# Cosine attention and a low-rank mixer: natural u of two batches by DMA transposes, an earlier mark for w_ch2, and seven more zero products

## The chip, the core and the metric

The kernel runs on one core of one Trainium2 chip. The time is device microseconds from the first to the last instruction, with what lies around it. Three timed runs of the kernel before took 311.78, 313.64 and 314.64 us (median 313.64). The profile is of one further execution.

TensorE multiplies matrices, VectorE and ScalarE do elementwise work and copies, GpSimd (POOL) some casts and the queue of the weight loads and most output writes, and SyncE (SP) issues nearly all other DMAs. Each engine works through its own instructions in order. DMA transposes are issued from SP.

## What is computed

Eight batches of attention with 8 heads, 576 positions and 64 features, in linear form with cosine weights, and then a mixer:

```python
q_p, k_p = phi(q, cos_w, sin_w), phi(k, cos_w, sin_w)   # relu, times cos and sin: 128 features
kv  = einsum('bhsf,bhsd->bhfd', k_p, v)
num = einsum('bhsf,bhfd->bhsd', q_p, kv)
den = einsum('bhsf,bhf->bhs', q_p, k_p.sum(axis=2))[..., None] + 1e-6
x   = (num / den).transpose(0, 2, 1, 3).reshape(8, 576, 512)

h   = x.transpose(0, 2, 1) @ U @ V            # rank 32, over positions
u   = x + h.transpose(0, 2, 1)
out = u + relu(u @ w_ch1) @ w_ch2             # 512 -> 2048 -> 512
```

Inputs and output are float32; products run in bfloat16 with float32 sums.

## The kernel before

**Tiling.** The 576 positions of a batch are four chunks of 128 (c = 0 to 3) and a tail of 64 (c = 4). The tails of two batches share one tile. The channel product of a batch therefore has 16 slots of g1 (`g1_main`: one block of 128 hidden channels by 512 positions, four matmuls into `g_ps`, ScalarE's relu into `hid`), and for each pair of batches there are four slots of g1 for the tails (`g1_tail`) and 36 slots of g2 (`g2_part`: nine position chunks in four parts, four matmuls into `o_ps` each; after the last part VectorE adds u from `u_bf` into `o_sb`, and it is written out).

**u is needed twice.** Transposed (`uT`, channels on partitions) it is the moving operand of g1. Natural (`u_bf`, positions on partitions) it is the term added to the output at the end of g2. For batches 2 to 7, `u_unit` makes natural u (one matmul of V by A into `va_ps`, and VectorE's add of x), and `utr_dma` (line 455) makes `uT` of it with DMA transposes. For batches 0 and 1, which have no earlier work to hide such a transfer behind, `uT` is made straight in PSUM: `uTd_open` or `open_mm` multiplies x by the identity, `uTd_mm` adds the product of A and V, and `uTd_evac` copies the sum as bfloat16 to `uT`. Natural u of these two batches is then also made by `u_unit`, from the same x and A.

**Order.** It is written out by hand as a list of slots; thunks placed with `at(j, ...)` or `put(j, ...)` are issued after slot j. Slots 0 to 15 are g1 of batch 0, 16 to 31 the early g2 of batch 0 (part by part over four chunks), 32 to 47 g1 of batch 1, 48 to 51 the tails, 52 to 71 the rest of g2 of the first pair. Attention of the next batches is laid beside these slots; `PLAN` (line 624) gives for batches 2 to 7 where q, k and v are prepared, where `kv_unit`, `x_unit`, `A_unit` and `u_unit` go and where the next batch's loads are issued. Attention of batch 1 lies beside slots 0 to 45, that of batch 2 has its kv products at slots 46 and 48, that of batch 3 at 60 and 62.

**Natural u of batches 0 and 1.** Lines 853 to 854 put the four chunks of batch 0 after slots 5 to 8. Lines 874 to 875 put the tail pair's chunk after slot 32 and the four chunks of batch 1 after slots 42 to 45. PSUM buffers are those with the tag "o" (two).

**Queues.** SP issues, in this order: the loads of q, k and v of batches 0 and 1; at slot 15 a tiny DMA that reads `w2_bf` (`gate`, line 842, and line 898), so that SP waits there until the second quarter of w_ch2 has landed; the loads of batch 2; the transposes `uT_tl` (slot 33) and those of q of batch 2 (`qtr_dma`, slots 36 to 40); the loads of batch 3, and so on. POOL's queue loads w_ch1 and w_ch2 in four quarters each. A small copy on POOL ahead of each (lines 814 and 825) reads `vst`, so that POOL waits until v of batch 0, or of batch 1, has landed (the first half of its heads):

```python
G_.tensor_copy(out=mark, in_=vst[0:TS, 3, 4, 0:1])
for n in range(4):
    w2_load(n)
```

**The head.** Before q of batch 0 has landed, TensorE multiplies zeros (`keep_warm`, line 191; 13 products at line 790) into a buffer that nothing reads.

**Buffers that the change touches.** `uT` and `x_bf` have two buffers each, `u_bf` three.

Of the kernel before, what the change touches and what calls it, by code (L numbers as in the profile page):

```python
# [11 lines left out]
BF16 = mybir.dt.bfloat16  # L12
# [5 lines left out]
def kernel(  # L18
# [11 lines left out]
    nc = tc.nc  # L30
# [6 lines left out]
    P = 128  # L37
    DM = 512
# [4 lines left out]
    TS = 64  # L43
# [5 lines left out]
    def tail(b):  # L49
        lo = TS * (b % 2)  # L50
        return slice(lo, lo + TS)

    const = ctx.enter_context(tc.tile_pool(name="const", bufs=1))
    pool = ctx.enter_context(tc.tile_pool(name="work", bufs=2))
# [6 lines left out]
    kst = const.tile([P, H, 5, D], FP32)  # L61
    vst = const.tile([P, H, 5, D], FP32)
# [4 lines left out]
    def load_even(dst, src, b, h0=0, h1=H):  # L67
        nc.sync.dma_start(
            out=dst[0:P:2, h0:h1].rearrange("m h c d -> m h (c d)"),
            in_=nines(src, b)[:, h0:h1, 0 : 5 * D],  # L70
        )
# [20 lines left out]
    w2_bf = const.tile([P, NJ, DM], BF16)  # L92
# [20 lines left out]
    V_, A_, G_ = nc.vector, nc.scalar, nc.gpsimd  # L113
# [15 lines left out]
    def load_uv():  # L129
# [16 lines left out]
        out=iota[:, 0:4], pattern=[[2, 4]], base=0, channel_multiplier=9,  # L146
        allow_small_or_imprecise_dtypes=True,
    )
    for lo in (0, TS):
        nc.gpsimd.iota(  # L150
            out=iota[lo : lo + TS, 4:5], pattern=[[1, 1]], base=8, channel_multiplier=18,
# [3 lines left out]
        out=iota[:, 5:6], pattern=[[1, 1]], base=8, channel_multiplier=9,  # L155
# [6 lines left out]
        out=par, in_=ident[:, 1:P:2], op=ALU.add, axis=mybir.AxisListType.X  # L162
    )
    V_.tensor_scalar(
        out=iota[:, 0:4], in0=iota[:, 0:4], scalar1=par, scalar2=None, op0=ALU.add
# [24 lines left out]
    def keep_warm(n, tag, bufs):  # L190
        w_ps = ps.tile([P, 512], FP32, tag=tag, bufs=bufs, name="w_ps")
        for _ in range(n):
            nc.tensor.matmul(out=w_ps, lhsT=zero[:, 0:P], rhs=zero, start=True, stop=True)  # L193
# [3 lines left out]
    mark = const.tile([TS, 1], FP32)  # L197
# [36 lines left out]
    u_bf, u_tl, uT, uT_tl = {}, {}, {}, {}  # L234
# [51 lines left out]
    def k_of(b, c, h):  # L286
        return k_p[b][:, c, h, :] if c < 4 else k_tl[:, h, :]
# [20 lines left out]
    def qT_alloc(b):  # L308
        if b not in q_pT:
            q_pT[b] = pool.tile([P, 4, H, P], BF16, tag="q_pT", bufs=2, name="q_pT")  # L310
# [48 lines left out]
    def x_of(b, c, rows=slice(0, P)):  # L359
        return x_bf[b][:, c, :] if c < 4 else x_tl[rows, :]  # L360
# [22 lines left out]
    def x_unit(b, c, tag, bufs):  # L383
        x_alloc(b)
        n = P if c < 4 else TS
        rows = slice(0, P) if c < 4 else tail(b)
        acc = ps.tile([P, 2, 512], FP32, tag=tag, bufs=bufs, name="x_ps")
        for h in range(H):
            g, i = divmod(h, 4)
            nc.tensor.matmul(  # L390
                out=acc[:, g, i * E : i * E + E],
                lhsT=qT_of(b, c, h),
                rhs=kv_sb[b][:, h, :],
                start=True,
                stop=True,
            )
        view = acc[rows, :, 0 : 4 * E].rearrange("p g (i e) -> p g i e", e=E)
        rec = pool.tile([P, 2, 4], FP32, tag="rec", bufs=2, name="rec")
        recip(rec[rows], view[:, :, :, D])
        nc.vector.tensor_tensor(  # L400
            out=x_of(b, c, rows).rearrange("p (g i d) -> p g i d", g=2, d=D),
            in0=view[:, :, :, 0:D],
            in1=rec[rows].unsqueeze(3).to_broadcast([n, 2, 4, D]),
            op=ALU.mult,
        )

    def A_of(b):
        return A_sb[b % 4]
# [19 lines left out]
    def u_unit(b, c, tag, bufs):  # L428
        if b not in u_bf:
            u_bf[b] = pool.tile([P, 4, DM], BF16, tag="u_bf", bufs=3, name="u_bf")  # L430
        if c == 4:
            u_tl[b // 2] = pool.tile([P, DM], BF16, tag="u_tl", bufs=2, name="u_tl")
        va = ps.tile([P, DM], FP32, tag=tag, bufs=bufs, name="va_ps")
        if c < 4:
            nc.tensor.matmul(out=va, lhsT=V_bf[:, c, :], rhs=A_of(b), start=True, stop=True)  # L435
        else:
            for i in range(2):
                nc.tensor.matmul(  # L438
                    out=va[tail(i), :], lhsT=V_tl, rhs=A_of(b - 1 + i), start=True, stop=True,
                    tile_position=(0, i * TS),  # L440
                )
        nc.vector.tensor_tensor(  # L442
            out=u_bf[b][:, c, :] if c < 4 else u_tl[b // 2], in0=x_of(b, c), in1=va,
            op=ALU.add,
        )
# [9 lines left out]
    def utr_dma(b, c0, c1):  # L455
        if c0 < 4:
            uT_alloc(b)
            nc.sync.dma_start_transpose(
                out=uT[b][:, c0:c1, :, :].rearrange("m c d t -> m (c d) t"),
                in_=u_bf[b][:, c0:c1, :].rearrange("p c n -> p (c n)"),  # L460
            )
        else:
            uTt_alloc(b // 2)
            nc.sync.dma_start_transpose(out=uT_tl[b // 2], in_=u_tl[b // 2])

    uT_ps = {}

    def uTd_open(b, d, tag, bufs, t=None):
# [134 lines left out]
    def loads(b):  # L603
        def thunk(dst, src):
            def go():
                load_tail(dst, src, b)
                load_main(dst, src, b)

            return go

        return thunk(qst, q), thunk(kst, k), thunk(vst, v)

    ORD = (4, 0, 1, 2, 3)
# [58 lines left out]
    O2, G3 = ("o", 2), ("g", 3)  # L672
# [114 lines left out]

    FEATS = [(V_, V_ if c == 3 else A_) for c in TL]
    qT_alloc(0)
    keep_warm(13, "X", 1)  # L790
    t_q = []
    for c in TL:
        tg = G3 if c < 3 else O2
# [10 lines left out]
    for c in TL:  # L804
        k_prep(0, c, FEATS[c])
        for h in range(H):
            nc.tensor.matmul(
                out=z_ps[:, h : h + 1], lhsT=k_of(0, c, h), rhs=v_tl[:, 0, D:E],
# [13 lines left out]
    for h0 in (0, 4):  # L822
        load_odd(vst, v, 1, h0, h0 + 4)
        load_even(vst, v, 1, h0, h0 + 4)
    G_.tensor_copy(out=mark, in_=vst[0:TS, 3, 4, 0:1])
    for n in range(4):
        w2_load(n)
    g1_main(0, 0, True)
# [10 lines left out]
    def at(j, *thunks):  # L839
        beside.setdefault(j, []).extend(thunks)  # L840

    def gate(src):
        nc.sync.dma_start(out=mark2, in_=src)

    for n, c in enumerate(ORD):
# [4 lines left out]
        at(9 + n, lambda c=c: k_prep(1, c, (V_, A_)))  # L850
        at(15, lambda c=c, n=n: v_prep(1, 0, H, (c,), ((V_, V_, V_, V_, V_)[n],)))
        at(18 + 2 * n, lambda c=c: x_unit(1, c, "X", 1))
    for c in range(4):
        at(5 + c, lambda c=c: u_unit(0, c, *O2))
    for hg in range(2):
        at(16 + hg, lambda hg=hg: kv_unit(1, hg, "T", 1))

# [13 lines left out]
    at(27, lambda: A_unit(1, "T", 1, A_))  # L871
    at(28, open1)
    at(29, close1)
    for n, c in enumerate(ORD):
        at((32, 42, 43, 44, 45)[n], lambda c=c: u_unit(1, c, *O2))
    at(33, lambda: utr_dma(1, 4, 5))

    slots, todo = [], {}
# [16 lines left out]
    def put(at, thunk):  # L895
        todo.setdefault(at, []).append(thunk)

    put(15, lambda: gate(w2_bf[0:1, 4, 0:1]))
    for n, t in enumerate(loads(2)):
        put(15, t)  # L900
# [37 lines left out]
```

## Time and profile before

| what | value |
|---|---|
| timed runs | 311.78, 313.64, 314.64 us (median 313.64) |
| profiled execution, whole | 311.89 us |
| its span | 310.1 us |
| g2 products (`o_ps`, line 576) | 40% of the chain of waits |
| g1 products (`g_ps`, line 523) | 32% of the chain |
| natural-u products (`va_ps`, line 435), 32 in all | 2% of the chain |
| natural-u adds on VectorE (line 442), 32 in all | 21.8 us busy, 685 ns each |
| w_ch2 quarters, POOL's issues | 33.9 to 36.9 us |
| SP's small DMA on w_ch2 (line 843) | issued at 42.90 us |
| loads of batch 2, first issue | 43.77 us |

The page gives busy time by engine, the span in 40 slices of 7.75 us, the DMA queues, the chain that ended last, and groups of instructions with the idle time before them. Lines with "<-" in brackets name what ended an engine's idle time. A timeline line has start, duration, engine, line, operation, output and inputs, and how many were merged; SPq is SP's queue of DMA issues, and its durations are those of issuing, not of the transfer. PEld is the load of a matmul's weights, which overlaps the matmuls.

### The profile page before, as it was taken

How to read it: one execution, taken by the hardware profiler on the slowest of the kernel's cores; microseconds unless marked ns; L12 is line 12 of the kernel's file. 1: busy time of each engine (PE TensorE's matmuls, PEld its weight loads, DVE VectorE, ACT ScalarE, POOL GpSimd, SP SyncE). 2: the span in 40 equal slices, each digit the busy share in tenths (PEclk: the TensorE clock that was granted, in tenths of full speed). 3: DMA queues.
4: the chain of work that ended last, by engine and by line, in shares of the span. 5: the costliest groups of instructions: out<-in, count | busy, mean ns of one | idle time of the engine just before them, and what ended most of it. 6: DMA issues, size and time to landing. Idle time of an engine off the chain costs nothing.

```text
span 310.1 us, 5750 instructions
## 1 busy us (share of the span) xinstructions
PE 301.9 (97%) x2341; PEld 157.7 (51%) x2341; DVE 155.0 (50%) x342; ACT 136.0 (44%) x229; POOL 52.9 (17%) x96
## 2 busy tenths in 40 slices
PE   5999999999999999999999999999999999999995
PEld 1676454446655444574455444574455444474443
DVE  4979834896878584146327583046426520002111
ACT  2936730264820466679300366669300366640000
POOL 8410400510131008004221300003321000000000
PEclk9999999999999999999999999999999999999999
DMA  7999999979997979982999879912981240001131
GB/s 216 354 258 255 197 187 274 326 143 241 288 191 142 314 133 251 243 242 82 180 212 322 207 127 234 273 47 53 194 154 60 75 80 0 0 2 68 70 101 68
DMA packets 86027, 53.21 MB, mean 172 GB/s; under 512 B 54258, under 2 KB 83218, under 8 KB 86002
## 3 DMA queue, kind: packets, MB, share of 16 engines
q1 hardware_dynamic: 79298, 41.36, 57.5%
q0 software_dynamic: 6560, 11.43, 15.0%
q8 instruction: 18, 0.29, 0.4%
q10 hardware_dynamic: 144, 0.07, 0.1%
q14 instruction: 7, 0.06, 0.0%
HBM read 36.86 MB, written 9.44 MB: 149 GB/s over the span
## 4 chain that ended last, share of the span: by engine, by line
PE 90%; DVE 5%; DMA 2%; issue 1%; ACT 0%; ACTq 0%; DVEq 0%
PE o_ps L576 40%; PE g_ps L523 32%; PE gt_ps L543 5%; PE kv_ps L299 3%; PE x_ps L390 3%; PE va_ps L435 2%; DMA qst<-in_q_dram 2%; DVE q_p L260 2%; DVE k_p L260 2%; PE a_ps L415 1%; PE t_ps L328 1%; PE t_ps L316 1%; PE w_ps L193 0%; PE va_ps L438 0%; PE xh_ps L688 0%
## 5 line engine op out<-in xcount | busy, mean ns | idle before, releaser
L532 ACT ACTIVATE hid<-g_ps 128x512 bf16<-128x512 f32 x128 | 76.2, 598 | 106.2 <-PE g_ps L523 106.2
L576 PE MATMUL o_ps<-w_bf,hid 128*128 128x512 bf16 (+2 forms) x528 | 120.0, 372 | 0.0
L523 PE MATMUL g_ps<-uT,w_bf 128*128 128x512 bf16 x512 | 117.6, 379 | 0.0
L523 PEld LDWEIGHTS <-w_bf 128*128 128x128 bf16 x512 | 48.9, 98 | 58.0 <-issue 2.1
L576 PEld LDWEIGHTS <-hid 128*128 128x128 bf16 x528 | 48.2, 98 | 50.8 <-issue 0.8
L586 DVE TENSOR_TENSOR o_sb<-u_bf,o_ps 128x512 f32<-128x512 bf16 (+2 forms) x33 | 22.1, 669 | 56.3 <-PE o_ps L576 56.2
L597 POOL DMA_DIRECT2D out_dram<-o_sb x24 | 15.2, 633 | 126.2 <-DVE o_sb L586 67.0
L442 DVE TENSOR_TENSOR u_bf<-x_bf,va_ps 128x512 bf16<-128x512 bf16 x32 | 21.8, 685 | 10.0 <-PE va_ps L435 9.9
L110 POOL CAST v_ext<-vst 128x512 bf16<-128x512 f32 (+1 forms) x28 | 20.1, 744 | 37.1 <-DMA vst<-in_v_dram 36.9
L110 DVE CAST kv<-kv_ps 128x260 bf16<-128x260 f32 (+1 forms) x15 | 6.4, 429 | 36.9 <-PE kv_ps L299 36.9
L400 DVE TENSOR_TENSOR x_bf<-x_ps,rec 128x512 bf16<-128x512 f32 x28 | 19.4, 691 | 1.0
L363 DVE TENSOR_SCALAR rec<-x_ps 128x8 f32<-128x8 f32 (+1 forms) x35 | 5.8, 165 | 22.8 <-PE x_ps L390 22.3
L543 PE MATMUL gt_ps<-uT_tl,w_bf 128*128 128x128 bf16 x256 | 15.9, 219 | 0.0
L260 DVE TENSOR_SCALAR q_p<-qst,cosw 128x512 bf16<-128x512 f32 x24 | 13.7, 583 | 2.9 <-DMA qst<-in_q_dram 2.9
L543 PEld LDWEIGHTS <-w_bf 128*128 128x128 bf16 x256 | 14.7, 98 | 0.9
L576 PE MATMUL o_ps<-w_bf,hid_tl 128*128 128x512 bf16 x64 | 14.8, 379 | 0.0
L390 PEld LDWEIGHTS <-q_pT 128*128 128x128 bf16 x224 | 10.7, 98 | 6.4 <-DVE x_bf L400 0.4
L258 ACT ACTIVATE k_p<-kst,sinw 128x512 bf16<-128x512 f32 x19 | 13.3, 712 | 0.0
L299 PEld LDWEIGHTS <-k_p 128*128 128x128 bf16 x256 | 11.1, 97 | 3.2 <-issue 0.3
L550 ACT ACTIVATE hid_tl<-gt_ps 128x512 bf16<-128x512 f32 x16 | 9.6, 597 | 6.6 <-PE gt_ps L543 6.6
L435 PE MATMUL va_ps<-A_sb,V_bf 128*128 128x512 bf16 x32 | 12.1, 379 | 0.1
L390 PE MATMUL x_ps<-kv,q_pT 128*128 128x65 bf16 x224 | 11.8, 194 | 0.0
(128 smaller groups left out, 233.0 us busy)
## 6 DMA issues: line engine op xcount, KB each, us to landing
qst<-in_q_dram SPq DMA_DIRECT2D x14, 512.0 KB, 6.3
kst<-in_k_dram SPq DMA_DIRECT2D x14, 512.0 KB, 8.6
vst<-in_v_dram SPq DMA_DIRECT2D x12, 512.0 KB, 8.1
out_dram<-o_sb POOLq DMA_DIRECT2D x24, 256.0 KB, 3.7
w_bf<-in_moe_w_ch_dram POOLq DMA_DIRECT2D x8, 512.0 KB, 11.1
out_dram<-o_sb SPq DMA_DIRECT2D x7, 256.0 KB, 2.4
qst<-in_q_dram SPq DMA_DIRECT2D x2, 640.0 KB, 6.4
kst<-in_k_dram SPq DMA_DIRECT2D x2, 640.0 KB, 10.8
```

Source lines behind the costliest of these rows:

```text
L110: eng.tensor_copy(out=o, in_=i)
L260: eng.tensor_scalar(out=o, in0=i, scalar1=0.0, scalar2=w, op0=ALU.max, op1=ALU.mult)
L299: nc.tensor.matmul(out=acc[:, i, :], lhsT=k_of(b, c, h), rhs=v_tl[:, h, 0:n] if c == 4 and b < 2 else vx[:, c, h, 0:n], start=(c == 0), st ...
L390: nc.tensor.matmul(out=acc[:, g, i * E : i * E + E], lhsT=qT_of(b, c, h), rhs=kv_sb[b][:, h, :], start=True, stop=True,)
L400: nc.vector.tensor_tensor(out=x_of(b, c, rows).rearrange("p (g i d) -> p g i d", g=2, d=D), in0=view[:, :, :, 0:D], in1=rec[rows].unsqueez ...
L435: nc.tensor.matmul(out=va, lhsT=V_bf[:, c, :], rhs=A_of(b), start=True, stop=True)
L442: nc.vector.tensor_tensor(out=u_bf[b][:, c, :] if c < 4 else u_tl[b // 2], in0=x_of(b, c), in1=va, op=ALU.add,)
L523: nc.tensor.matmul(out=g_ps.rearrange("p (c t) -> p c t", c=4), lhsT=w1_bf[:, d, j * P : j * P + P], rhs=uT[b][:, :, d, :], start=(d == 0) ...
L532: nc.scalar.activation(out=hid[b][:, j, :], in_=g_ps, func=AF.Relu, bias=0.0, scale=1.0)
L543: nc.tensor.matmul(out=g_ps[:, jj, :], lhsT=w1_bf[:, d, j * P : j * P + P], rhs=uT_tl[pr][:, d, :], start=(d == 0), stop=(d == 3),)
L576: nc.tensor.matmul(out=o[:, cols], lhsT=lhs[:, j, c * P : c * P + P], rhs=w2_bf[:, j, cols], start=(j == 0), stop=(j == NJ - 1),)
L586: nc.vector.tensor_tensor(out=o_sb[:, cols], in0=u[:, cols], in1=o[:, cols], op=ALU.add)
```

## The change

Natural u of batches 0 and 1 (not the tail pair) is no longer computed by `u_unit`. A new function `u_dma` issues a DMA transpose of two chunks of `uT` into `u_bf`; two calls make a batch. Batch 0's two go to slot 15, behind a new small DMA that waits for the first quarter of w_ch2 and ahead of the one that waits for the second quarter and of batch 2's loads. Batch 1's two go to slot 31, on SP ahead of `uT_tl`, of batch 2's q transposes and of batch 3's loads. The tail pair's `u_unit` stays at slot 32. The copy that holds POOL ahead of w_ch2 reads the last-loaded part of k of batch 1 in place of v. The head has 20 zero products in place of 13.

```diff
+    def u_dma(b, c0, c1):
+        if b not in u_bf:
+            u_bf[b] = pool.tile([P, 4, DM], BF16, tag="u_bf", bufs=3, name="u_bf")
+        nc.sync.dma_start_transpose(
+            out=u_bf[b][:, c0:c1, :].rearrange("t c (d n) -> t (c d) n", n=P),
+            in_=uT[b][:, c0:c1, :, :].rearrange("n c d t -> n (c d t)"),
+        )
...
-    keep_warm(13, "X", 1)
+    keep_warm(20, "X", 1)
...
-    G_.tensor_copy(out=mark, in_=vst[0:TS, 3, 4, 0:1])
+    G_.tensor_copy(out=mark, in_=kst[0:TS, 7, 4, 0:1])
     for n in range(4):
         w2_load(n)
...
-    for c in range(4):
-        at(5 + c, lambda c=c: u_unit(0, c, *O2))
...
-    for n, c in enumerate(ORD):
-        at((32, 42, 43, 44, 45)[n], lambda c=c: u_unit(1, c, *O2))
+    at(32, lambda: u_unit(1, 4, *O2))
+    for c0 in (0, 2):
+        at(31, lambda c0=c0: u_dma(1, c0, c0 + 2))
     at(33, lambda: utr_dma(1, 4, 5))
...
+    put(15, lambda: gate(w2_bf[0:1, 0, 0:1]))
+    for c0 in (0, 2):
+        put(15, lambda c0=c0: u_dma(0, c0, c0 + 2))
     put(15, lambda: gate(w2_bf[0:1, 4, 0:1]))
     for n, t in enumerate(loads(2)):
         put(15, t)
```

## The prediction

> **What bounds the kernel now.** I read the page's busy table and its 40 slices first: they say which engine sets the end and whether its clock is whole.
>
> ```profile
> PE 301.9 (97%) x2341; PEld 157.7 (51%) x2341; DVE 155.0 (50%) x342; ACT 136.0 (44%) x229; POOL 52.9 (17%) x96
> ...
> PE   5999999999999999999999999999999999999995
> ...
> PEclk9999999999999999999999999999999999999999
> DMA  7999999979997979982999879912981240001131
> ```
>
> TensorE is busy in every slice at full granted clock, so what leaves its queue should shorten the span unless something new makes it wait. The DMA engines are full up to slice 8 (62 us). The chain of waits, piece by piece, shows the products that the change removes:
>
> ```profile
> 30.46 0.22 PE va_ps L435
> 30.68 0.86 PE g_ps L523 x4
> ...
> 70.48 0.61 DVE u_bf L442
> 71.09 0.04 issue
> 71.13 0.38 PE va_ps L435
> ```
>
> A natural-u product costs 0.22 us on the chain (its row's 379 ns is the pipelined length), and for batch 1 VectorE's add stood between two of them. Next the timeline of SP's queue, where the new transposes go, and the line of the existing transposes of the same size:
>
> ```profile
> 52.11 1.30 SPq L81 DMA_DIRECT2D vst<-in_v_dram  x1
> 61.10 1.32 SPq L464 DMA_TRANSPOSE uT_tl<-u_tl  x1
> 62.52 1.21 SPq L347 DMA_TRANSPOSE q_tlT<-q_tl  x1
> 64.97 4.32 SPq L342 DMA_TRANSPOSE q_pT<-q_p  x2
> 69.35 1.09 SPq L87 DMA_DIRECT2D qst<-in_q_dram  x1
> ```
> ```profile
> L458 SPq DMA_TRANSPOSE uT<-u_bf x12: 1231/1232/1882, 94.1 to 251.1; - x12
> ...
> DMA to landing us min/median/max: 3.0/3.3/4.9
> ```
>
> SP has a hole from 53.4 to 61.1, just where batch 1's transposes enter. Last, the place where an earlier TensorE meets an unmoved engine, from the timelines of ScalarE and the weight loads:
>
> ```profile
> 86.28 1.14 ACT L108 ACTIVATE v_ext<-vst 128x512 bf16<-128x512 f32 x2
> ```
> ```profile
> 88.58 0.18 PEld L299 LDWEIGHTS <-k_p 128*128 128x128 bf16 x4 [0.27 <-issue]
> ```
>
> Batch 3's v is ready at 87.42 and its kv products begin at 88.58: 1.16 us of slack.
>
> **Removed products.** Eight 128x512 products go, at slots 5 to 8 and 42 to 45: 8 x 0.216 (0.864 per group of four) = 1.73 us, all on the chain. The wait at 70.9 goes too: that piece is 0.38 instead of 0.22, so 0.16. Gross gain 1.89. The eight adds (0.69 each, 5.5 us) lie beside TensorE and give nothing more: before 34 us VectorE already idles 0.39 between them. After 70 us their place is taken by the kv evacuations, which follow TensorE. What is late next at slot 46 is batch 2's k: VectorE's chain of q and k ends at 70.48. It starts behind the o_sb add at 59.01, which moves 0.86 with TensorE, so it ends about 69.6. The kv products are then due at 73.08 - 1.9 = 71.2; 1.6 us remain.
>
> **Four transposes on SP.** Each has the form of L458 (eight 128x128 blocks): 1.23 us of SP and 3.0 to landing when the queue is free. The nearest loaded row is the second pair of q_pT at 82.46, twice the blocks, 8.48 us for two: so 1.23 to 4.24 each. Their DMA time: around 246 to 256 us the shares 0.23, 0.46 and 0.34 over 2.9, 3.6 and 3.5 us make 3.5 us of all engines for 20 blocks, or 1.4 for each new transpose.
>
> Batch 0's pair waits for w_ch2's first quarter at slot 15. Behind it on SP stand the second mark and the nine loads of batch 2. The loads went out from 43.77; with the mark about 38 and the pair taking 2.5 to 8.5 they go out between 42 and 48 (each mark 0.75). Their users are later: qst landed 7.2 us after its last issue at 45.19, so 52.4, and VectorE takes it at 59.6; kst landed near 57.5 and is taken at 66.45; vst at 60.8, used by TensorE at 73.3. Cover of 7, 9 and 12 us: cost nothing, and 0 to 1 if all of it were late by the worst 4. u of batch 0 itself is wanted at 54.66 - 0.86 and lands by 48.
>
> Batch 1's pair can go out at about 57.9 (both engines' copies of uT end at 58.67, less 0.86), into SP's hole. Behind it: uT_tl, q_tlT, q_pT, then the loads of batch 3. Unloaded it ends at 60.4 and delays uT_tl by 0.2. Issued behind v loads that land at 60.8 it may take 3 to 4 us: uT_tl goes out at 62, q_tlT at 63.3, q_pT at 64.5 where its data would allow 64.1. I take 0.4 us of delay for batch 3's loads, because the L458 rows lie between 1.23 and 1.88 and only q_pT's are longer; bounds 0 to 4.8 (8.5 us for the pair, from 57.9).
>
> That delay is paid at 88.58. TensorE arrives 1.9 earlier, at 86.7. ScalarE's k and v casts of batch 3 take 6.05 us from the landing of k (81.2; the cast began at 81.37). SP moves 0.86 earlier less 0.4, so v is ready at 87.42 - 0.46 = 86.96: a stall of 0.3. Bounds: none if SP is not delayed, 4.7 with 4.8 us.
>
> The Trainium skill speaks against this trade: "VectorE: DVE Perf Modes", The three transpose paths, gives 1309 ns for a 128x128 block through DMA and 390 on TensorE and advises TensorE. By that, one block after another, a transpose would be 10.5 us (an estimate), batch 1's pair would hold batch 3's loads for over 10 us, and the sum would be a loss. L458 lands eight blocks in 3.0 us, so here blocks overlap and the trace decides.
>
> **w_ch2 released by k.** The mark waits for k's last rows (issued 15.11, 13.8 to landing: 28.9) instead of v's first half (33.46). Four POOL issues move from 33.9 to about 29.2; POOL has nothing else there. They are behind w_ch1 in the same queue, whose last quarter lands at 15.6 + 19.5 = 35.1, so the first quarter of w_ch2 lands at perhaps 38 (39.8 before; quarters follow at 2.0 to 2.7 us). It is needed: the weight load at 39.83 waited 0.4 for it, and TensorE now comes at 39.1. Unmoved it would cost 0.7; I take 0. v's second half landed at 35.9 and shares the engines; VectorE casts it in 1.84 and kv wants it at 39.6, so it may be almost 2 us late. Cost 0, bounds 0 to 1.
>
> **Twenty zero products.** The thirteen end at 5.51 and q's first transpose starts at 8.15. The later ones follow at about 0.2, so seven more add 1.5 and end at 7.0: nothing. If all ran at the early spacing of 0.43, twenty would end at 9.8, 1.6 too late; if in some executions TensorE were at half clock when q comes, the 3.8 us of work between 8 and 12 could stretch by as much. In this trace it is not: at 8.61, after 2.64 us idle, a zero product takes 0.38. Bounds -3 to +1.6, taken as 0.
>
> By the Trainium skill, "TensorE: Matmul & The Clock Gate", Part 1, the moment of the switch varies from run to run, so one trace can't show all; by it the seven could save some runs part of a half-clock stretch.
>
> **The sum.** -1.73 - 0.16 + 0.3 = -1.6 us. The profiled execution took 311.89 (span 310.1), so 310.3 on its scale. It is near the lowest of the three timed (311.78, 313.64, 314.64; median 313.64). The middle of all four is 312.8; from there 311.2.
>
> **The rivals.**
> - *The head gains too.* For: two executions lie 1.9 and 2.8 above the lowest, about a late clock in the head. Against: the trace shows none. It would give 311.2 - 2 = 309.2. Chance 0.21.
> - *SP clogs.* Both new pairs cost what the pair of q_pT at 82.46 did. Batch 1's holds SP from 57.9 to 66.4; uT_tl and q_tlT go to 68.9, q_pT to 73.2, batch 3's loads begin at 73.3, 4 late; v ready 91.4 against 86.7, a stall of 4.7: 312.8 - 1.9 + 4.7 = 315.6. It makes a loss once batch 3's v is over 1.2 us later than now, when the stall (from 86.7) has eaten all 1.9. For: DMA is full to 62 us and gets 5.6 us more. Against: eight blocks only, and the share falls to 0.44 from 62 to 66. Chance 0.11.
> - *The gain is eaten at slots 12 to 17.* w_ch2 and v share bandwidth, or w_ch1's last quarter (35.1, wanted at 35.6) slips, and TensorE waits 0.7 to 1.5: 312.3. Chance 0.13.
>
> **How the numbers follow.** Forecast 0.55: 310.3 to 312.2. About what a measurement can tell is 1%, 3.1 us here. Faster by over 1% is the first rival and a little of the forecast: 0.24. Slower by over 1% needs a give-back near 5: 0.09. The range runs from the head's 309.0 to 313.9, which takes in the eaten gain and half of the start of the clogged case.
>
> **What would show it.** Right: no va_ps at 30 or 69 us, TensorE 0.86 earlier at 40 and 1.9 at 73, uT_tl issued by 62, batch 3's kv within 0.5 us of its turn. Wrong: a TensorE wait for w_bf near 39, for v_ext or k_p at 87, SP blocked past 64, or a zero product ending after q has landed.

## The result, and the profile after

| | before | after |
|---|---|---|
| median of 22 runs each | 313.69 us | 314.93 us |
| lowest to highest | 311.78 to 315.85 | 313.62 to 317.65 |
| profiled execution: time, span | 311.89, 310.1 | 313.78, 312.0 |
| ratio after to before, 95% interval | | 1.0059 [1.0037, 1.0081] |

The ratio of the two kernels' runs makes the change 0.6% slower, some 1.9 us; the medians differ by 1.24 us and the two profiled executions by 1.89. 1.6 us less had been forecast. 314.93 lies above the range of 309.0 to 313.9. The busy table and the slices of the page of the changed kernel, in the rows that the prediction showed of before:

```profile
PE 302.7 (97%) x2340; PEld 158.0 (51%) x2340; DVE 147.0 (47%) x334; ACT 136.0 (44%) x229; POOL 54.7 (18%) x96
...
PE   8999999999789999999999999999999999999995
...
PEclk9999999999999999999999999999999999999999
DMA  7999999999995999992899699912891140001131
```

TensorE has a gap that it did not have: the digits 7 and 8 in the eleventh and twelfth slice, 78 to 94 us. The DMA engines are full up to slice 12, four slices longer than before. What stood before the gap is read from the chain of waits (start, duration, what); this is its stretch from SP's q transposes of batch 2 to the kv products of batch 3:

```profile
68.87 3.56 SPq L342
72.43 0.05 issue
72.49 0.62 SPq L87
...
78.10 1.62 SPq L74
79.72 0.04 issue
79.76 5.86 DMA vst<-in_v_dram
85.62 3.68 ACT k_p L258 x6
89.30 1.05 ACT v_ext L108 x2
90.35 0.04 issue
90.39 0.67 PE kv_ps L299 x17
```

Read from below: the kv products begin at 90.39 because ScalarE's casts of batch 3 end there, those because its loads land late, and those because SP issues them late. The loads took no longer than before: they went out 3.14 us later, and v was ready 2.92 us later (90.34 against 87.42). Ahead of the first line the chain passes to VectorE's work on q and k of batch 2, but SP did not wait for that: the last q row ended at 63.56 and SP took up these transposes at 66.61. Why SP is late stands in the timeline of its queue in the changed kernel:

```profile
39.40 5.27 SPq L469 DMA_TRANSPOSE u_bf<-uT  x2
...
57.95 5.83 SPq L469 DMA_TRANSPOSE u_bf<-uT  x2
63.87 1.30 SPq L464 DMA_TRANSPOSE uT_tl<-u_tl  x1
65.26 1.25 SPq L347 DMA_TRANSPOSE q_tlT<-q_tl  x1
66.61 5.82 SPq L342 DMA_TRANSPOSE q_pT<-q_p  x2
72.49 0.62 SPq L87 DMA_DIRECT2D qst<-in_q_dram  x1
```

Batch 1's pair of transposes holds SP from 57.95 to 63.78. `uT_tl` follows 2.77 us later than before, and the first load of batch 3 goes out at 72.49, 3.14 later. The line of the new transposes (durations of the issue in ns, then time to landing):

```profile
L469 SPq DMA_TRANSPOSE u_bf<-uT x4: 1355/2875/3889, 39.4 to 59.9; - x4
...
DMA to landing us min/median/max: 7.7/8.0/8.9
```

The form is that of L458, of which the prediction showed 1.23 us of issue and 3.0 to landing. Here, between loads in flight, the first of a pair takes 1.36 (batch 0) and 1.89 us (batch 1) and the second up to 3.9, and each lands after about 8. The price of the delay is in the timelines of VectorE and of TensorE (in brackets: idle time before, and what ended it):

```profile
80.24 0.49 DVE L260 TENSOR_SCALAR q_p<-qst,cosw 128x512 bf16<-128x512 f32 x1 [2.46 <-DMA qst<-in_q_dram]
```
```profile
82.22 0.43 PE L390 MATMUL x_ps<-kv,q_pT 128*128 128x65 bf16 x8 [1.84 <-DVE x_bf L400]
...
89.67 0.39 PE L299 MATMUL kv_ps<-v_ext,k_p 128*128 128x65 bf16 x2 [0.36 <-POOL v_ext L110]
90.39 0.19 PE L299 MATMUL kv_ps<-v_ext,k_p 128*128 128x65 bf16 x1 [0.33 <-ACT v_ext L108]
```

First VectorE waits 2.46 us for q of batch 3. It works in order, so `rec` and `x_bf` of batch 2 stand behind that wait and TensorE's x product of batch 2 waits for `x_bf`. Ten us further on it waits for v of batch 3, cast by POOL and by ScalarE. The same products' starts in the two executions give the whole account:

| product | before | after | after minus before | lost since the row above |
|---|---|---|---|---|
| first x product of batch 2 from `q_pT` | 80.06 | 78.23 | -1.83 | |
| second, behind eight g2 products | 82.04 | 82.22 | +0.18 | 2.01 |
| fourth | 86.11 | 86.47 | +0.36 | 0.18 |
| first kv product of batch 3 | 88.58 | 89.11 | +0.53 | 0.17 |
| g2 products behind that kv group | 89.20 | 90.90 | +1.70 | 1.17 |

Up to 78 us the change had gained 1.83 us, or 2.00 counted from the first product of g1, which came 0.17 later in this execution (22.63 against 22.46). In the next 13 us it lost 3.53, and the rest of the span adds 0.2.

### The profile page after: what moved, and what is told of

Read it like the earlier page. It is cut to its first block, busy times and chain, and to the rows that moved or that the text cites. A ratio compares the mean times of both kernels' runs of the same rounds, so it can differ in the third digit from the quotient of the medians.

```text
span 312.0 us, 5752 instructions
## 1 busy us (share of the span) xinstructions
PE 302.7 (97%) x2340; PEld 158.0 (51%) x2340; DVE 147.0 (47%) x334; ACT 136.0 (44%) x229; POOL 54.7 (18%) x96
## 4 chain that ended last, share of the span: by engine, by line
PE 84%; DVE 4%; SPq 4%; DMA 4%; ACT 2%; issue 1%; ACTq 0%; DVEq 0%
PE o_ps L584 37%; PE g_ps L531 31%; PE gt_ps L551 3%; PE kv_ps L299 3%; PE x_ps L390 2%; DMA vst<-in_v_dram 2%; DMA qst<-in_q_dram 2%; DVE k_p L260 2%; PE va_ps L435 2%; SPq L342 2%; ACT k_p L258 1%; DVE q_p L260 1%; SPq L74 1%; SPq L87 1%; PE t_ps L328 1%
## 5 line engine op out<-in xcount | busy, mean ns | idle before, releaser
L531 PE MATMUL g_ps<-uT,w_bf 128*128 128x512 bf16 x512 | 116.4, 379 | 0.0
L110 POOL CAST v_ext<-vst 128x512 bf16<-128x512 f32 (+1 forms) x28 | 21.9, 806 | 38.3 <-DMA vst<-in_v_dram 33.7
L442 DVE TENSOR_TENSOR u_bf<-x_bf,va_ps 128x512 bf16<-128x512 bf16 x24 | 16.5, 686 | 8.8 <-PE va_ps L435 8.8
L260 DVE TENSOR_SCALAR q_p<-qst,cosw 128x512 bf16<-128x512 f32 x24 | 11.2, 479 | 5.4 <-DMA qst<-in_q_dram 5.4
L299 PE MATMUL kv_ps<-v_ext,k_p 128*128 128x65 bf16 (+1 forms) x256 | 12.2, 193 | 0.8 <-POOL v_ext L110 0.4
```

What stands on the lines that cost most here:

```text
L110: eng.tensor_copy(out=o, in_=i)
L260: eng.tensor_scalar(out=o, in0=i, scalar1=0.0, scalar2=w, op0=ALU.max, op1=ALU.mult)
L299: nc.tensor.matmul(out=acc[:, i, :], lhsT=k_of(b, c, h), rhs=v_tl[:, h, 0:n] if c == 4 and b < 2 else vx[:, c, h, 0:n], start=(c == 0), st ...
L442: nc.vector.tensor_tensor(out=u_bf[b][:, c, :] if c < 4 else u_tl[b // 2], in0=x_of(b, c), in1=va, op=ALU.add,)
L531: nc.tensor.matmul(out=g_ps.rearrange("p (c t) -> p c t", c=4), lhsT=w1_bf[:, d, j * P : j * P + P], rhs=uT[b][:, :, d, :], start=(d == 0) ...
```

## The experiments

The theories: **A**, batch 1's pair on SP makes batch 3's loads late, and VectorE's q and ScalarE's v of batch 3 with them. **B**, batch 0's pair does it: with its wait for w_ch2 it puts off batch 2's loads (45.52 against 43.77) and what follows them on SP. **C**, the seven further zero products, for good or ill. And for the mark of w_ch2: **M1**, reading k in place of v changes nothing; **M2**, without it TensorE would wait for w_ch2 near 40 us; **M3**, the earlier w_ch2 takes bandwidth from v of batch 1. "Before" and "after" are the two kernels, and edits are against the changed kernel unless said. Each ratio is to runs of the kernel before on the same chip, with a 95% interval.

**1. Batch 1's pair behind batch 3's loads.**

```diff
-    for c0 in (0, 2):
-        at(31, lambda c0=c0: u_dma(1, c0, c0 + 2))
...
+    for c0 in (0, 2):
+        put(43, lambda c0=c0: u_dma(1, c0, c0 + 2))
```

> Batch 1's two u transposes go from slot 31 to slot 43, on SP behind batch 3's loads; all else as in the changed kernel. Theory A (batch 1's pair holds SP for 5.8 us and makes batch 3's loads 3.1 us late, for which TensorE waits 3.7 us at 80 to 82 and 89 to 90): the first load of batch 3 goes out at 68.5 to 69.5 instead of 72.5, and both waits go; the pair is then ahead of batch 3's q transposes and may cost 0 to 2.5 us near 99, before g1 of batch 2. Ratio to before 0.994 to 1.002. Theory B (batch 0's pair is the root: it makes batch 2's loads late, and everything behind them): the loads of batch 3 still start after 71, ratio 1.003 or more.

Measured: 312.71 us, 0.9974 [0.9939, 1.0009]. Batch 3's loads begin at 69.67, although this execution's head is 1.85 us later than that of after, and TensorE waits only 0.3 us at 86 (for `x_bf`) and 0.2 at 89. The pair takes 6.60 us of SP at 79.70, behind the loads, and the q transposes and `uT` of the next batches follow later without a wait of TensorE. Batch 0's pair is still there, and the loss goes away with the place of batch 1's pair alone: A.

**2. Batch 1's natural u on TensorE again.** Batch 0's pair, the mark by k and 20 zero products stay.

```diff
-    at(32, lambda: u_unit(1, 4, *O2))
-    for c0 in (0, 2):
-        at(31, lambda c0=c0: u_dma(1, c0, c0 + 2))
+    for n, c in enumerate(ORD):
+        at((32, 42, 43, 44, 45)[n], lambda c=c: u_unit(1, c, *O2))
```

> Natural u of batch 1 is made by products again (slots 42 to 45); batch 0's pair, the k mark and the 20 zero products stay. Theory A: SP is free again, batch 3's loads start near 69, the waits at 80 and 89 go, and 0.86 us (four products) remains gained: ratio 0.996 to 0.999. Theory B: batch 3's loads start after 71 and the ratio is 1.002 or more.

Measured: 311.58 us, 0.9958 [0.9931, 0.9985]: faster than both kernels. SP's timeline in this run, to be set against that of after:

```profile
60.38 1.21 SPq L464 DMA_TRANSPOSE uT_tl<-u_tl  x1
61.69 1.22 SPq L347 DMA_TRANSPOSE q_tlT<-q_tl  x1
63.00 6.18 SPq L342 DMA_TRANSPOSE q_pT<-q_p  x2
69.23 0.62 SPq L87 DMA_DIRECT2D qst<-in_q_dram  x1
```

Batch 3's loads are back at 69.23, and TensorE waits nowhere near 80 or 89. A again: batch 0's pair alone costs TensorE nothing. One thing more is to be seen: the q transposes begin 2 us earlier than before (63.00 against 64.97) and end at the same time (69.18 against 69.29), for their issue takes 6.18 in place of 4.32. An earlier SP did not bring the loads earlier. The earlier start has a cause of its own, which the prediction did not see, in the first q row of batch 2 on VectorE and the casts of v on POOL, in before and in this run:

```profile
61.00 2.76 DVE L260 TENSOR_SCALAR q_p<-qst,cosw 128x512 bf16<-128x512 f32 x1
60.63 2.85 POOL L110 CAST v_ext<-vst 64x512 bf16<-64x512 f32 x5
```
```profile
60.28 0.53 DVE L260 TENSOR_SCALAR q_p<-qst,cosw 128x512 bf16<-128x512 f32 x1
65.13 4.56 POOL L110 CAST v_ext<-vst 128x512 bf16<-128x512 f32 x4 [4.60 <-DMA vst<-in_v_dram]
```

In before one VectorE operation lasts 2.76 us beside POOL's five casts, and q of batch 2 is ready 2.2 us later for it. In all five profiles without batch 0's pair (before, 3, 6, 9 and 12) it takes 2.74 to 2.76, in the ten with it 0.47 to 0.75 us: the pair puts off the loads of batch 2, and four of the casts come later (in experiments 1 and 13 four rows beside them take 0.82 or 0.83 each). Why the two delay each other no run shows.

**3. Batch 0's natural u on TensorE again**, batch 1's by DMA as in the change.

```diff
+    for c in range(4):
+        at(5 + c, lambda c=c: u_unit(0, c, *O2))
...
-    put(15, lambda: gate(w2_bf[0:1, 0, 0:1]))
-    for c0 in (0, 2):
-        put(15, lambda c0=c0: u_dma(0, c0, c0 + 2))
```

> Natural u of batch 0 is made by products again (slots 5 to 8), and its pair and the first mark leave SP; batch 1's pair stays at slot 31. Theory A: the pair still takes 4 to 6 us of SP and batch 3's loads start near 72; the 0.86 us of added products are taken from TensorE's wait, so the ratio stays at 1.004 to 1.008. Theory B: the pair falls to 2.5 to 3.8 us, batch 3's loads start by 70, ratio 0.996 to 1.001.

Measured: 313.99 us, 1.0018 [0.9986, 1.0050], between the ranges of A and B, a miss for both as written; its interval takes in parts of both. The row of the new transposes in this run:

```profile
L469 SPq DMA_TRANSPOSE u_bf<-uT x2: 1357/1491/1625, 59.0 to 60.4; - x2
...
DMA to landing us min/median/max: 4.3/4.9/5.4
```

Without batch 0's pair the loads of batch 2 begin at 41.73 (45.52 in after). Batch 1's pair then holds SP for 3.03 us, not 5.83, and batch 3's loads go out at 71.46. That is only one us earlier than in after, because the pair itself goes out one us later (58.99) and `uT_tl` behind it takes 2.13 in place of 1.30. TensorE still waits 1.4 us for v near 90. Batch 0's pair, harmless by itself, thus makes batch 1's dearer: 5.68 to 5.93 us in the four profiles that have both at these places (after, 4, 8, 11), 3.03 here and 3.15 in experiment 6. The likely reason is that it moves batch 2's loads towards the time of that pair.

**4. Thirteen zero products** in the changed kernel.

```diff
-    keep_warm(20, "X", 1)
+    keep_warm(13, "X", 1)
```

> 13 zero products in place of 20, all else as in the changed kernel. Theories A and B: nothing in the head waits for them (they end at 7.5, q's first transpose starts at 8.16), so the ratio stays at 1.004 to 1.008. Theory C (the seven products cost the head time, or turn some runs slow): the ratio falls by 0.003 or more.

Measured: 315.07 us, 1.0058 [1.0029, 1.0088], the same as after. By the time alone they are worth nothing. The profile shows something else. Its windows (length, busy time with counts of TensorE, weight loads, VectorE, ScalarE, POOL, then granted clock, DMA share, GB/s):

```profile
80.00:84.00 4.00, 1.69 (x15) 0.76 (x14) 2.36 (x7) 1.32 (x2) 0.00 (x0) 1.00 1.14 289
84.00:86.00 2.00, 2.00 (x8) 0.81 (x7) 1.93 (x6) 0.00 (x0) 0.00 (x0) 0.73 1.15 221
86.00:88.00 2.00, 2.00 (x13) 1.03 (x12) 1.81 (x6) 1.92 (x4) 0.61 (x1) 0.50 1.10 339
```

TensorE has stood 0.65 us until 79.09 and 2.31 us for `x_bf` until 83.55, and soon afterwards its granted clock is 0.50 for some 3.4 us: eight products of 128x512 that begin at 86.60 keep the next one waiting until 89.18, 2.58 us, where such a group otherwise takes 1.73 to 1.74. In this execution, then, the stall costs again by the clock.

**5. Experiment 2 with the mark reading v as before.**

```diff
-    G_.tensor_copy(out=mark, in_=kst[0:TS, 7, 4, 0:1])
+    G_.tensor_copy(out=mark, in_=vst[0:TS, 3, 4, 0:1])
```

> The kernel with batch 1's natural u made by products, batch 0's by its pair of transposes (it measured 0.9958), with w_ch2 again released by batch 1's v. Theory M1 (the earlier mark is not needed): TensorE finds w_ch2 in time and the ratio stays within 0.0015 of 0.9958. Theory M2 (it pays for the products saved at slots 5 to 8): TensorE waits 0.5 to 0.9 us for w_ch2 near 39, batch 2's loads go out 1 to 2 us later, ratio 0.997 to 1.000.

Measured: 312.87 us, 0.9984 [0.9956, 1.0011]. It lies 0.0026 above experiment 2, in the range of M2, but the intervals overlap, and its profiled execution is no help: the head is 2.4 us late, and TensorE comes after w_ch2 in any case. Inconclusive between M1 and M2.

**6. The kernel before with batch 1's pair added**: two transposes of `uT` of batch 1 into a tile that nothing reads, at the place on SP that the change gave them. Edit against before:

```diff
+    scratch = const.tile([P, 4, DM], BF16, name="scratch")
+    def u_copy(b, c0, c1):
+        nc.sync.dma_start_transpose(out=scratch[:, c0:c1, :]..., in_=uT[b][:, c0:c1, :, :]...)
...
+    for c0 in (0, 2):
+        at(31, lambda c0=c0: u_copy(1, c0, c0 + 2))
```

> The kernel before, all its products kept, plus two DMA transposes of batch 1's uT after slot 31 into a scratch tile that nothing reads: the cost of the pair by itself. Theory A (the pair holds SP): it takes 3 to 4 us of SP, batch 3's loads go out 1.5 to 2.5 us after 69.35, TensorE waits 0.4 to 1.4 us for batch 3's v; ratio 1.001 to 1.005. Theory B (it hurts only behind batch 0's pair): loads within 0.7 us of 69.35, ratio 0.998 to 1.001.

Measured: 314.69 us, 1.0029 [0.9995, 1.0063]. The pair takes 3.15 us of SP, batch 3's loads go out at 72.96, and with 1.74 us of that owed to a later head they are 1.9 later than before. ScalarE's k then waits 1.9 us for its load and TensorE 0.3 for kv. The delay is what A said, and the ratio lies in A's range, though its interval takes in 1 and TensorE's wait is a little under the 0.4 to 1.4 expected. The price is small, since the products that the change removes are still here and cover the rest.

**7. Batch 1's transposes split**: both batches by DMA, batch 1's first two chunks behind batch 3's loads, the others at slot 59, each ahead of its use.

```diff
-    for c0 in (0, 2):
-        at(31, lambda c0=c0: u_dma(1, c0, c0 + 2))
...
+    put(43, lambda: u_dma(1, 0, 2))
+    put(59, lambda: u_dma(1, 2, 4))
```

> The changed kernel with batch 1's pair split: chunks 0 and 1 behind batch 3's loads (slot 43), chunks 2 and 3 behind batch 3's q transposes (slot 59). Theory A (what stands behind each transpose on SP sets its price): batch 3's loads start at 68.5 to 70, no wait at 80 or 89, batch 3's q transposes are done 3 us earlier than with both at slot 43; ratio 0.993 to 0.998. Rival: the second transpose makes batch 2's uT late, TensorE waits 1 us or more near 99, and the ratio is 0.998 or more.

Measured: 311.23 us, 0.9952 [0.9918, 0.9985], the lowest median of the study, not to be told from experiment 2. SP's timeline:

```profile
64.21 5.06 SPq L342 DMA_TRANSPOSE q_pT<-q_p  x2
69.32 1.00 SPq L87 DMA_DIRECT2D qst<-in_q_dram  x1
...
78.66 4.03 SPq L469 DMA_TRANSPOSE u_bf<-uT  x1
...
92.41 1.44 SPq L469 DMA_TRANSPOSE u_bf<-uT  x1
93.95 4.33 SPq L458 DMA_TRANSPOSE uT<-u_bf  x2
```

Here all eight products are gone and the loads go out as before. A single transpose behind the loads takes 4.03 us of SP, and none of it reaches TensorE. In the chain of this run the kv products of batch 3 still follow on batch 3's v without a gap: there is no slack left at that place.

**8. Twice the suspected cost**: the changed kernel with two more transposes (of the same source, into a tile that nothing reads) behind batch 1's pair, by the `u_copy` of experiment 6.

```diff
     for c0 in (0, 2):
         at(31, lambda c0=c0: u_dma(1, c0, c0 + 2))
+    for c0 in (0, 2):
+        at(31, lambda c0=c0: u_copy(1, c0, c0 + 2))
```

> The changed kernel with two more transposes of batch 1's uT after slot 31, into a scratch tile that nothing reads: the suspected cost doubled. Theory A: batch 3's loads start 2.5 to 6 us after 72.5 and TensorE waits as much longer between 79 and 95; ratio to before 1.013 to 1.026. Rival (the added time comes from elsewhere, not from the loads behind the pair): ratio under 1.010.

Measured: 319.09 us, 1.0180 [1.0131, 1.0229]. SP's timeline and TensorE's waits (total, times, longest):

```profile
58.27 5.78 SPq L469 DMA_TRANSPOSE u_bf<-uT  x2
64.11 4.90 SPq L477 DMA_TRANSPOSE scratch<-uT  x2
...
77.31 0.77 SPq L87 DMA_DIRECT2D qst<-in_q_dram  x1
```
```profile
PE x_ps L390 <- DVE x_tl L400: 3.8, 1, 3.8
```

Batch 3's loads are 4.8 us later than in after, and the median of the four runs is 4.2 us longer: with the slack gone, more delay of these loads is paid in full size. How much of it is the delay alone is not separated, for behind the stall of 3.8 us, which ended at 82.49, TensorE's granted clock is 0.50 until about 91.6, and a group of eight products that spans 1.89 us elsewhere in the timeline spans 3.60 there.

**9. The kernel before with the mark reading k**, alone. Edit against before:

```diff
-    G_.tensor_copy(out=mark, in_=vst[0:TS, 3, 4, 0:1])
+    G_.tensor_copy(out=mark, in_=kst[0:TS, 7, 4, 0:1])
```

> The kernel before with the earlier mark for w_ch2 alone. Theory M1 (neither needed nor harmful there): w_ch2's first quarter lands 1 to 2 us earlier, v of batch 1 about 2 us later, both hidden, batch 2's loads 1 to 2 us earlier and nothing waits for them: ratio 0.998 to 1.002. Theory M3 (v of batch 1 becomes late, or POOL's issues slow VectorE): TensorE waits at 40 to 41 for batch 1's kv; ratio 1.002 or more.

Measured: 314.85 us, 1.0041 [1.0007, 1.0076]: slower, though little, a miss for M1 and in the range of M3. But the profile does not show the wait at 40 us that M3 named. It shows a late clock in the head: 0.63 and 0.52 in 8 to 10 and 10 to 12 us, a head 1.76 us late, and 10 of the 12 timed runs have a mean granted clock of 0.995 or less (12 of 23 of before beside them). Whether the mark brought that or the chance of these runs stays open.

**10. Experiment 7 with the mark reading v.** The edit of the mark is that of experiment 5.

> The split version (0.9952) with w_ch2 released by v again. Theory M1: no wait for w_ch2 beyond 0.3 us; batch 0's pair and batch 2's loads go out 2 to 3 us later, and batch 3's loads with them by under 1 us; ratio within 0.0015 of 0.9952. Theory M2: TensorE waits 0.5 us or more for w_ch2 near 39 (later by as much as the head is), or for batch 3's v near 87; ratio 0.997 to 1.001.

Measured: 311.83 us, 0.9981 [0.9945, 1.0016]. Here TensorE arrives before w_ch2, from the list of its waits:

```profile
PE o_ps L584 <- DMA w_bf<-in_moe_w_ch_dram: 0.7, 1, 0.7
```

That is the 0.7 us that the prediction put on an unmoved mark. The ratio, from another chip, differs from that of experiment 7 by 0.0029, inside the intervals: M2 is shown as a wait, and its size in the total is not.

**11 to 13. The zero products once more.** Experiment 4 spoke for nothing, but all runs together had shown low clocks more often in kernels with 13. On one chip: the changed kernel as it stands, before with 20, and experiment 7 with 13.

```diff
-    keep_warm(13, "X", 1)
+    keep_warm(20, "X", 1)
```

> The changed kernel once more, as it stands, as the yardstick of this chip for the two beside it. All theories: 1.004 to 1.008 of before. Theory A (the batch-1 pair delays batch 3's loads, TensorE stands still near 80 and 89 us) adds now: where TensorE has stood still near 80 us the granted clock of 84 to 90 us falls to a half in part of the executions, as it did with 13 zero products (0.50 in 86 to 88 us); so a mean clock of 0.995 or less in a third or more of the timed runs here.

> The kernel before with 20 zero products in place of 13, nothing else. Theory C1 (the seven more keep the granted clock up when q's transposes begin; half of the timed runs of the kernel before have a mean clock of 0.995 or less and are 2.05 us slower than the others by median, 314.23 against 312.18): the share of such runs falls from a half to a fifth or less, ratio 0.995 to 0.999. Theory C0 (nothing, as the comparison of 13 and 20 in the changed kernel said): the share stays near a half, ratio 0.999 to 1.001.

> The fastest version (batch 1's transposes split between slots 43 and 59) with 13 zero products. C1: half of the timed runs at a mean clock of 0.995 or less, ratio 0.997 to 1.000 instead of 0.9952. C0: ratio 0.994 to 0.997, share of low clocks no higher than the 2 of 12 that the version with 20 showed.

| run | zero products | median us | ratio | runs at a clock of 0.995 or less |
|---|---|---|---|---|
| 11, changed kernel | 20 | 314.44 | 1.0037 [1.0009, 1.0065] | 5 of 12 |
| 12, before | 20 | 312.55 | 0.9984 [0.9957, 1.0010] | 1 of 12 |
| 13, experiment 7 | 13 | 312.40 | 0.9958 [0.9927, 0.9989] | 8 of 12 |
| 7 | 20 | 311.23 | 0.9952 [0.9918, 0.9985] | 2 of 12 |
| before, beside 11 to 13 | 13 | 313.43 | | 14 of 29 |

With 20 the low clocks become rare in both pairs, as C1 said: 1 of 12 against 14 of 29, and 2 of 12 (on another chip) against 8 of 12. The other kernels with 20 that have no long stall near 80 us agree: 1 to 3 of 12 in experiments 1, 2, 3, 5 and 10. The windows of run 13 show where the low clock is:

```profile
8.00:10.00 2.00, 1.71 (x14) 1.43 (x15) 2.00 (x7) 2.00 (x4) 1.06 (x3) 0.60 1.08 349
10.00:12.00 2.00, 2.00 (x17) 1.54 (x16) 0.78 (x3) 1.10 (x2) 0.00 (x0) 0.54 1.08 355
12.00:14.00 2.00, 1.94 (x22) 1.31 (x21) 1.30 (x3) 1.42 (x2) 0.98 (x3) 1.00 1.09 358
```

In time it comes to 0.0016 in the one pair and 0.0006 in the other, and neither interval tells that from nothing. The changed kernel has 20 and still 5 of 12 low, and 13 of 22 in its first runs: its stall near 80 us, shown in experiments 4 and 8 to be followed by half clock, is the likely origin. It is not shown: no profile of a low run with 20 was taken, and in the profiles of after and of run 11, with stalls of 1.84 and 2.00 us, the clock from 80 to 92 us is 1.00.

## Why the prediction was wrong

**The step that failed** is "I take 0.4 us of delay for batch 3's loads". It was worked out from a pair of 3 to 4 us and from q transposes that take 4.32 us as before, and chosen because L458's issues lie between 1.23 and 1.88 us. Batch 1's pair took 5.83 (5.93 in run 11), so `q_pT` went out at 66.61 where the step had 64.5. And `q_pT` then took 5.82, a term that the step had left as it was; it is 5.73 to 5.90 in all five profiles with this one pair ahead of it (after, 3, 4, 6, 11). In the nine without the pair it is 4.32 to 6.46, so that the pair brings this lengthening is not shown. Of the error 2.1 us come from the pair and 1.5 from the q transposes behind it. Batch 3's loads went out 3.14 us later than before, where the step put them 0.46 earlier (0.86 from the earlier TensorE, less 0.4): the delay was 4.0 us in place of 0.4.

That lies inside the bounds that were given, 0 to 4.8; the choice between them went to the wrong row. L458's rows are taken from 94 us on, where the DMA share is 0.76 in the mean, against 1.08 from 40 to 94 us. The loaded row, 8.48 us for twice the blocks, was at hand and used for the upper bound alone. Two more parts of the working were wrong. Batch 2's loads were put among what batch 0's pair delays at no cost, but where they come later, batch 1's pair is longer: 5.83 against 3.03 (experiment 3) and 3.15 (experiment 6). And "SP moves 0.86 earlier" does not move the loads: in experiment 2 the q transposes began 2 us earlier and ended as before.

**The stall.** Put at 0.3, at kv; it was 3.5, in two places. That the delay "is paid at 88.58" named the second and smaller one. The first is at 80 us, where VectorE's q of batch 3 stands in its queue ahead of batch 2's `rec` and `x_bf`: a load that is late for batch 3 stops a product of batch 2. The prediction followed k and v of batch 3 and not q. The stall's error, 3.2 us, is nearly the whole error of the sum: -1.6 forecast, +1.9 measured in the profiled pair. In the absolute time 0.9 us more come from the starting point: 312.8 was taken for the kernel before, from four executions, and the median of 22 is 313.69.

**The rival "SP clogs"**, at 0.11, was the case that came. Its path holds: loads at 73.3 forecast and 72.49 measured, v ready at 91.4 and 90.34, a stall of 4.7 and 3.5, 315.6 us and 314.93. That the numbers came so near is in part luck: it took 8.5 us for the pair, which was 5.83, and left `q_pT` near 4.3, which was 5.82, and it too had the whole stall at kv. Its point of decision was v 1.2 us later than before; it came 2.9 later (90.34 against 87.42). Experiments 1, 2, 7 and 8 confirm the path by moving the pair, taking it away and doubling it. In chances, its weight was too small: the argument against it, a DMA share of 0.44 from 62 to 66 us, was read from a trace without the new transposes and with batch 2's loads early. In after it is 0.73 there, and 1.64 from 58 to 62 (1.06 before).

**Right.** The gross gain: 1.89 forecast, 1.83 at 78 us. The cover of batch 2's loads, which went out at 45.52 and made no product of TensorE wait. w_ch2 in time with the mark at k, and the 0.7 us that an unmoved one would cost TensorE (experiment 10). Zero products end at 7.48 (forecast 7.0), before q's transposes at 8.16. Batch 2's q and k on VectorE were in time too, by more than forecast: they ended at 67.53, not 69.6, since the row of 2.76 us shown under experiment 2 fell to 0.53.

**The zero products taken at 0** is not contradicted by a time, but by the clocks it is too little: fewer low clocks, in sizes of 0.16 and 0.06% that the intervals do not tell from nothing. The rival *The head gains too* was right in kind, by the clocks, and put at 2 us, more than any comparison here shows.

**The rival of slots 12 to 17** did not come: TensorE shows no wait for `w_bf` near 39 us, and batch 1's v, some two us later than before, was still cast in time for its kv products.

## What to carry to other kernels

Price a moved DMA at the queue's state where it goes, not at its best row, and count everything behind it in that queue: here 5.8 us of issue in front of the next batch's loads cost 3.5 us, more than the 1.8 us that all eight products had given. The place decided, not the trade: the same transposes behind those loads gave 0.9974, and split 0.9952, where ahead of them they gave 1.0059. When a load is late, look in every in-order engine for the first instruction that takes it, and for other work that stands behind that instruction.

## What the runs showed of the hardware

- The issue of a transpose is as long as the queue makes it. The same eight-block form took 1.23 us of SP and 3.3 to landing in the median of L458's rows of before, and up to 3.9 us and about 8 to landing behind loads in flight (up to 4.5 of SP in experiment 5). "VectorE: DVE Perf Modes", The three transpose paths, of the Trainium skill gives 1309 ns for a 128x128 block by DMA. Added up over eight blocks that would be 10.5 us (an estimate); the eight-block transposes here landed after 3.0 to 9.7 us, so blocks do not add up, least of all on a free queue. The same page's Rules for kernel authors advise TensorE for a 128x128 transpose where the result may go to PSUM. Here the DMA lost only where its pair held SP for 5.8 us ahead of loads that were waited for.
- Behind stalls of 2.31 us (experiment 4) and 3.77 us (experiment 8), TensorE's granted clock was 0.50 for about 3.4 and 10 us, in experiment 8 from just before the end of the stall on; after stalls of 1.84 and 2.00 us in the two profiled executions of the change it stayed at 1.00 (one profile each). A stall can cost a second time.
- In all five profiles without batch 0's pair one VectorE operation of 0.5 us takes 2.74 to 2.76 us beside five casts on POOL; in experiments 1 and 13 four rows each take 0.82 or 0.83 beside such casts.
- Executions differ by 2 us or more through the head alone. With the same head of 20 zero products, the first product of g1 begins at 22.42 to 25.02 us over ten profiles, with q's first load; with 13 a low clock from 8 to 12 us comes on top in some. So only places that are compared by their distance from it, or medians of many runs, tell kernels apart at this size.
